# Casting q and k of step 9 inside step 7's block, and loading v of step 10 behind step 9's transpose

## The chip, the cores and the metric

The kernel runs on one NeuronCore of one Trainium2 chip. The metric is the device time of one execution in microseconds (us). The kernel before was run six times: 205.12, 204.30, 204.86, 205.36, 204.22 and 204.88 us, so its median is 204.87 us. One further execution was recorded by the hardware profiler; all views of the profile come from that one.

## The reference

A decaying linear attention over blocks of 64 tokens is followed by a dense layer pair with a GELU between. Inputs are q, k and v (4 batches, 8 heads, 768 tokens, 64 features, float32), one decay `lam` per head, `w_in` (512 x 2048) and `w_out` (2048 x 512). The output is 3072 x 512 in float32.

```python
for b in range(nb):                      # blocks of 64 tokens
    intra = einsum('bhic,bhjc->bhij', qb, kb) * Dmask      # scores under the decay mask
    intra = einsum('bhij,bhjd->bhid', intra, vb)
    inter = einsum('bhid,bhde->bhie', qb * lam_pow, kv_state)
    out[block b] = intra + inter
    kv_state = lam**block * kv_state + einsum('bhsd,bhse->bhde', kb * rev_pow, vb)
x = out.transpose(0, 2, 1, 3).reshape(B * S, H * D)
h = x @ w_in
g = 0.5 * h * (1 + tanh(c * (h + 0.044715 * h**3)))
return g @ w_out
```

## The kernel before

**Steps.** The attention is cut into 24 steps, numbered 0 to 23. A step is one batch, 256 tokens and four of the eight heads; step 2i and step 2i + 1 hold the two halves of the heads for the same tokens, and three such pairs make up a batch. The 256 tokens of a step are treated as two chunks of 128 (called c = 0 and c = 1). What a step needs before its matmuls is made in these parts:

- `load_step(s)` issues three DMAs of 256 KB, for q, k and v of the step, from SyncE's queue (SP, line 69). Each of the three has four buffers. Steps 0 to 8 are loaded by the code at the top; from step 6 on, `prep_v(s)` ends with `load_ahead(s + 3)`, so `prep(6)` loads step 9, `prep(7)` step 10, `prep(8)` step 11 and `prep(9)` step 12.
- `prep_qk(s)` casts q to fp16 with its decay on VectorE (line 240) and k to fp16 on ScalarE (line 245). For steps from `FIRST_DMA_T = 9` on it then issues a DMA on SP that transposes both (line 249) into the tile `qkT`. Steps before 9 are transposed by TensorE in `stage_t` (line 261) and copied out of PSUM on ScalarE or VectorE.
- `prep_v(s)` casts v to fp16 with its decay on GpSimd (POOL, line 230). `prep(s)` is `prep_qk(s)` followed by `prep_v(s)`.

**Blocks.** `R(n, s)` puts out the matmuls of two steps that are one apart: `scores(n)` (q times k of step n, line 290, which reads `qkT` of step n); then `products(n, s)`, which is k times v of step n (line 325), masked scores times v of step s (line 339), and the carried state times q of step s (line 348), followed by the copies to `xT` on ScalarE (line 367); then `causal(n)`, the masking of step n's scores on VectorE (line 299); and `update(n, 0)`. `U(n)` is `update(n, 1)`. An `update(n, c)` adds to the state on VectorE (lines 384 and 387) and then spreads it into a tile `u` on POOL (line 394). The state matmuls of step s in `products(n, s)` read `u` of (s - 2, 1) for chunk 0 and `u` of (s, 0) for chunk 1.

**Filler.** Between the blocks, `fill(n)` puts out the next n pieces of the dense layers: matmuls with `w_in` into `Hps` (line 422) with a GELU on ScalarE (line 426), and the second layer's products `MA`, `MB`, `MC`, `MD` (line 493), which use sums of `gT` made on VectorE (line 469).

**Order.** Every instruction is pinned (`pin`): each engine, and SP's DMA queue, runs its own in the order of the code, and an instruction that waits holds up everything behind it on its engine. Around the change the code reads:

```python
    R(6, 5)
    ...
    R(7, 6)
    U(7)
    prep(9)
    fill(2)
    for n in range(8, NSTEP + 1):
        stage_t(n); prep(n + 2); fill(2); R(n, n - 1); fill(1); U(n); fill(2 or 3)
```

So on SP the order is: the load of step 9, a store of an output tile, the load of step 10, another store, the load of step 11, the transpose of step 9, the load of step 12, the transpose of step 10, the load of step 13. On POOL it is: the `u` tiles of step 7, v of step 9, v of step 10, the two `u` tiles of step 8, v of step 11. The `u` of (8, 0) is read in `R(9, 8)`, which also has the `scores(9)` that read the transpose of step 9.

Of the kernel before, what the change touches and what calls it, by code (L numbers as in the profile page):

```python
# [15 lines left out]
def kernel(  # L16
# [22 lines left out]
    FIRST_DMA_T = 9  # L39
# [18 lines left out]

    ld32 = {}

    def load_step(s):
        b, r = divmod(s, 2 * NSB)
        sb, half = divmod(r, 2)
        ts = []
        for nm, src in (("q", q), ("k", k), ("v", v)):
            t = ld.tile([P, HH, 2, D], FP32, tag=nm + "32", name=f"{nm}32_{s}")
            rows = src[b, half * HH : (half + 1) * HH, sb * SB : (sb + 1) * SB, :]
            queue = nc.scalar if (nm, s) == ("v", 0) else nc.sync
            pin(queue.dma_start(out=t[:].rearrange("p h j d -> p h (j d)"),  # L69
                                in_=rows.rearrange("h (p j) d -> p h (j d)", j=2)))  # L70
            ts.append(t)
        ld32[s] = ts

    w_in16 = w16p.tile([P, NC, DFF], FP16)
    w_out16 = w16p.tile([P, NF, DM], FP16)
# [67 lines left out]
    def load_ahead(s):  # L143
        if s < NSTEP:
            load_step(s)
# [50 lines left out]
    def odd(hs):  # L196
        pin(nc.vector.tensor_tensor(dq[:, hs, 1], dq[:, hs, 0], lam_bc[:, hs], ALU.mult))

    def inverse(hs):
        pin(nc.vector.reciprocal(dv[:, hs], dq[:, hs]))  # L200
# [16 lines left out]
    def prep(s):  # L217
        prep_qk(s)
        prep_v(s)

    def wide(t):
        return t.rearrange("p j h d -> p h j d")

    def decay(t, s):
        hs = halves[s % 2]
        return t[:, hs, :].unsqueeze(3).to_broadcast([P, HH, 2, D])

    def prep_v(s):
        tv = a16p.tile([P, 2, HH, D], FP16, tag="v16", name=f"v16_{s}")
        pin(nc.gpsimd.tensor_tensor(wide(tv[:]), ld32[s][2][:], decay(dv, s), ALU.mult))  # L230
        a16[s] = a16[s] + (tv,)
        if s >= 6:
            load_ahead(s + 3)

    def prep_qk(s):
        q32, k32, _ = ld32[s]
        tqk = a16p.tile([P, 2, 2, HH, D], FP16, tag="qk16", name=f"qk16_{s}")
        tq, tk = tqk[:, 0], tqk[:, 1]
        q_eng = nc.gpsimd if s == 3 else nc.vector
        pin(q_eng.tensor_tensor(wide(tq), q32[:], decay(dq, s), ALU.mult))  # L240
        if s == 0:
            inverse(halves[0])
            odd(halves[1])
            inverse(halves[1])
        pin(nc.scalar.activation(out=wide(tk), in_=k32[:], func=AF.Copy))  # L245
        a16[s] = (tq, tk)
        if s >= FIRST_DMA_T:
            o = qkp.tile([P, 2, 2, 2, P], FP16, tag="qkT", name=f"qkT_{s}")
            pin(nc.sync.dma_start_transpose(out=o[:].rearrange("p a j h t -> p (a j h) t"),
                                            in_=tqk[:].rearrange("p a j h d -> p (a j h d)")))  # L250
            qkT[s] = o

    def stage_t(s):
        if s >= FIRST_DMA_T:
            return
        tq, tk = a16[s][:2]
        Tps = ps_M.tile([P, 2, 2, 2, P], FP16, tag="M", name="Tps")
        for i, t in enumerate((tq, tk)):
            for hp in range(2):
                for j in range(2):  # L260
                    pin(nc.tensor.transpose(Tps[:, i, j, hp, :], t[:, j, 2 * hp : 2 * hp + 2, :],  # L261
                                            ident[:]))
        o = qkp.tile([P, 2, 2, 2, P], FP16, tag="qkT", name=f"qkT_{s}")
        if s in (2, 3):
            pin(nc.scalar.activation(out=o[:, 0], in_=Tps[:, 0], func=AF.Copy))
            pin(nc.vector.tensor_copy(out=o[:, 1], in_=Tps[:, 1]))
        elif s in (1, 5, 6, 8):
            pin(nc.scalar.activation(out=o[:], in_=Tps[:], func=AF.Copy))
        else:
            pin(nc.vector.tensor_copy(out=o[:], in_=Tps[:]))  # L270
        qkT[s] = o
# [7 lines left out]
    def half64(i):  # L279
        return slice(64 * i, 64 * i + 64)  # L280
# [3 lines left out]
    def scores(n):  # L284
        o = qkT[n]
        Sps = ps_S.tile([P, 2, 2, 2, P], FP32, tag="S", name="Sps")
        for hp in range(2):
            for jk in range(2):
                for hl, c in TILES:
                    pin(nc.tensor.matmul(  # L290
                        Sps[half64(c), hl, hp, jk, :], o[half64(hl), 1, jk, hp, half64(c)],
                        o[half64(hl), 0, :, hp, half64(c)], start=True, stop=True,
                        skip_group_check=True))
        Ss[n] = Sps

    def causal(n):

        t = ptp.tile([P, 2, 2, 2, P], FP16, tag="PT", name=f"PT_{n}")
        pin(nc.vector.tensor_tensor(  # L299
            t[:].rearrange("p a b c d -> p (a b) (c d)"),  # L300
            Ss.pop(n)[:].rearrange("p a b c d -> p (a b) (c d)"),
            mask[:].unsqueeze(1).to_broadcast([P, 4, 2 * P]), ALU.mult))
        PTs[n] = t

    def products(n, s, banks=None, evacuate=True):


        OK, opened = banks or ([ps_M.tile([P, 512], FP32, tag="M", name=f"OK{c}")
                                for c in range(2)], set())

        def start(c, hl):
            if (c, hl) in opened:
                return False
            opened.add((c, hl))
            return True

        if n is not None:
            _, tk, tv = a16[n]
            last = (n // 2) % NSB == NSB - 1
            for jk in range(2):  # L320
                for hp in range(2):
                    for c, hl in TILES:
                        if c == 1 and last:
                            continue
                        pin(nc.tensor.matmul(  # L325
                            OK[c][half64(hl), 256 + hp * D : 256 + hp * D + D],
                            tk[half64(c), jk, 2 * hp + hl, :], tv[half64(c), jk, 2 * hp + hl, :],
                            start=start(c, hl), stop=(jk == 1), skip_group_check=True))
            Kps[n] = OK
        if s is None:  # L330
            return OK, opened
        sbg, half = divmod(s, 2)
        o = qkT.pop(s)
        PT = PTs.pop(s)
        _, _, tv = a16.pop(s)
        for hp in range(2):
            for jk in range(2):
                for c, hl in TILES:
                    pin(nc.tensor.matmul(  # L339
                        OK[c][half64(hl), hp * P : hp * P + P], tv[half64(c), jk, 2 * hp + hl, :],  # L340
                        PT[half64(c), hl, hp, jk, :], start=start(c, hl), stop=False,
                        skip_group_check=True))
        for c in range(2):
            if c == 0 and sbg % NSB == 0:
                continue
            u = us.pop((s, 0) if c else (s - 2, 1))
            for hp in range(2):
                pin(nc.tensor.matmul(OK[c][:, hp * P : hp * P + P], u[:, hp].rearrange("p l d -> p (l d)"),  # L348
                                     o[:, 0, :, hp, half64(c)], start=False, stop=True,
                                     skip_group_check=True))  # L350
        if evacuate:
            x_out(s, OK)
        return OK, opened

    def x_out(s, OK, second=None):
        sbg, half = divmod(s, 2)
        g, i = group_of[sbg]
        if g not in xT:
            xT[g] = xtp.tile([P, 2, len(groups[g]), 2, SB], FP16, tag="xT", name=f"xT_{g}")
        dst = xT[g][:, half, i]  # L360
        for c in range(2):
            d = dst[:, :, c * P : (c + 1) * P].rearrange("p hp (t j) -> p hp j t", j=2)
            o = OK[c][:, 0:256].rearrange("p (hp j t) -> p hp j t", hp=2, j=2)
            if c == 1 and second is not None:
                pin(second.tensor_copy(out=d, in_=o))
            else:
                pin(nc.scalar.activation(out=d, in_=o, func=AF.Copy))  # L367
# [228 lines left out]
        for _ in range(min(n, len(filler))):  # L596
            filler.pop(0)()

    def R(n, s):
        if n is not None:  # L600
            scores(n)
        products(n, s)
        if n is not None:
            causal(n)
        if s is not None and s % 2 == 1:
            g, i = group_of[s // 2]
            if i == len(groups[g]) - 1 and g > 0:
                queue_group(g)
        if n is not None:
            update(n, 0)  # L610
# [94 lines left out]
    sum_wout(1, 1, DVE)  # L705
    sum_wout(1, 7, DVE)
    fill(2)
    R(7, 6)
    U(7)
    prep(9)  # L710
    fill(2)

    for n in range(8, NSTEP + 1):
# [41 lines left out]
```

## Time and profile before

| | value |
|---|---|
| median of six runs | 204.87 us |
| the profiled execution, its own time | 205.59 us |
| its span in the trace | 203.8 us |
| TensorE matmul busy | 195.1 us (96%) |
| VectorE busy | 145.1 us (71%) |
| ScalarE busy | 108.3 us (53%) |
| GpSimd busy | 66.2 us (32%) |
| transposes by DMA | 15, median 4.6 us from issue to landing |
| loads of q, k, v from SP | 71, medians 4.9, 4.8 and 5.3 us |

Times in the views are microseconds from the start of the span. A timeline row gives start, duration, engine, line, operation, written tile and read tile, how often (x), and in brackets the idle time before it with what ended that. In the chain of waits, each row is a piece of the work that ended last, in order of time. SPq marks an instruction that issues a DMA; its duration is that of the issue, and the landing is told apart. The granted TensorE clock is 1.00.

### The profile page before, as it was taken

The page shows a single profiled execution, that of the slowest core. Times are in us where ns is not written, and L with a number is a line of the kernel's source. Part 1 is how long each engine was busy: PE and PEld are TensorE (multiplying, and loading weights), DVE is VectorE, ACT ScalarE, POOL GpSimd, SP SyncE. Part 2 cuts the span into 40 slices and gives each one's busy share as a digit, 9 for nine tenths or more (in the row PEclk, how much of TensorE's full clock was granted, in tenths as well). Part 3 has the DMA queues.
Part 4 walks back from the last instruction along what each step waited for, and adds up shares of the span by engine and source line. Part 5 has one row for each costly group of instructions (what it writes and reads, how often), then busy time and mean ns, then how long its engine had stood idle before and what let it go on. Part 6 is the DMA issues. An engine that isn't in the chain of part 4 may idle for free.

```text
span 203.8 us, 5650 instructions
## 1 busy us (share of the span) xinstructions
PE 195.1 (96%) x2348; PEld 129.8 (64%) x2348; DVE 145.1 (71%) x281; ACT 108.3 (53%) x205; POOL 66.2 (32%) x80
## 2 busy tenths in 40 slices
PE   6979999999996999999999999999999999999993
PEld 1556544456885888644688654688554788544882
DVE  5896624889999778939997828996739763226553
ACT  3465777375874473477723377632476431566210
POOL 6594132457473533146044304224413101000000
PEclk9999999999999999999999999999999999999999
DMA  6999999999999999599459985775240003300014
GB/s 173 290 330 388 383 387 374 291 285 279 323 244 213 271 250 292 132 272 209 55 157 193 299 191 146 78 177 149 67 106 0 3 0 106 105 0 0 3 42 164
DMA packets 64201, 37.85 MB, mean 186 GB/s; under 512 B 17584, under 2 KB 59568, under 8 KB 64176
## 3 DMA queue, kind: packets, MB, share of 16 engines
q1 hardware_dynamic: 63344, 36.97, 71.3%
q10 hardware_dynamic: 832, 0.52, 0.9%
q8 instruction: 18, 0.29, 0.6%
q14 instruction: 7, 0.06, 0.1%
HBM read 27.26 MB, written 6.29 MB: 165 GB/s over the span
## 4 chain that ended last, share of the span: by engine, by line
PE 81%; DMA 8%; SPq 4%; DVE 3%; ACT 2%; issue 1%
PE Hps L422 36%; PE MD L493 8%; PE MB L493 8%; PE MA L493 7%; PE MC L493 4%; DMA qkT<-qk 4%; SPq L69 4%; DMA wi<-in_moe_w_in_dram 4%; PE Hps L539 3%; PE Sps L290 3%; PE O2ps L437 3%; PE OK L348 3%; PE OK L339 2%; DVE w_sum L128 2%; PE Tps L261 1%; PE OK L325 1%
## 5 line engine op out<-in xcount | busy, mean ns | idle before, releaser
L422 PE MATMUL Hps<-xT,w_in 128*128 128x512 f16 (+1 forms) x416 | 79.1, 346 | 0.0
L426 ACT ACTIVATE gT<-Hps 128x512 f16<-128x512 f32 x88 | 52.1, 597 | 24.5 <-PE Hps L422 23.6
L422 PEld LDWEIGHTS <-w_in 128*128 128x128 f16 x416 | 40.3, 98 | 33.2
L394 POOL TENSOR_TENSOR u<-t,lumask 128x256 f16<-128x256 f32 x40 | 29.2, 734 | 81.9 <-DVE t L387 59.4
L469 DVE TENSOR_TENSOR gs<-gT 128x512 f16<-128x512 f16 (+1 forms) x74 | 43.0, 641 | 12.7 <-ACT gT L426 12.6
L493 PEld LDWEIGHTS <-gs 128*128 128x128 f16 x400 | 38.7, 98 | 4.4
L299 DVE TENSOR_TENSOR PT<-Sps,mask 128x1024 f16<-128x1024 f32 x24 | 29.2, 1216 | 14.5 <-PE Sps L290 14.5
L230 POOL TENSOR_TENSOR v<-v,dv 128x512 f16<-128x512 f32 x24 | 28.7, 1194 | 6.4 <-DMA v<-in_v_dram 2.8
L367 ACT ACTIVATE xT<-OK 128x256 f16<-128x256 f32 x47 | 18.1, 455 | 19.2 <-PE OK L348 15.8
L500 ACT ACTIVATE m<-MB 128x512 f32<-128x512 f32 x10 | 6.0, 597 | 26.5 <-PE MB L493 26.5
L493 PE MATMUL MA<-w_sum,gT 128*128 128x256 f16 x160 | 19.5, 273 | 0.1
L245 ACT ACTIVATE qk<-k 128x512 f16<-128x512 f32 x24 | 15.0, 626 | 8.3 <-DMA k<-in_k_dram 7.0
L493 PE MATMUL MD<-w_sum,gs 128*128 128x256 f16 x152 | 19.4, 273 | 0.0
L493 PE MATMUL MB<-w_out,gs 128*128 128x256 f16 x160 | 19.1, 273 | 0.0
L493 PEld LDWEIGHTS <-gT 128*128 128x128 f16 x160 | 15.5, 98 | 3.1 <-ACT gT L426 0.5
L240 DVE TENSOR_TENSOR qk<-q,dq 128x512 f16<-128x512 f32 x23 | 16.4, 717 | 0.0
L504 DVE TENSOR_TENSOR o<-MA,m 128x512 f32<-128x512 f32 x10 | 6.9, 685 | 12.0 <-ACT m L500 12.0
L387 DVE SCALAR_TENSOR_TENSOR t<-t,lamu,OK 128x64 f32<-128x64 f32 x64 | 14.7, 272 | 0.6
L437 PE MATMUL O2ps<-w_out,gT 128*128 128x512 f16 x64 | 14.6, 379 | 0.0
L128 DVE TENSOR_TENSOR w_sum<-w_out 128x1024 f16<-128x1024 f16 x10 | 9.0, 936 | 6.3 <-POOL w_out L118 3.5
L290 PEld LDWEIGHTS <-qkT 64*64 64x64 f16 x384 | 6.1, 106 | 10.0 <-issue 4.7
L290 PE MATMUL Sps<-qkT 64*64 64x128 f16 x384 | 10.0, 222 | 2.1 <-DMA qkT<-qk 1.6
(59 smaller groups left out, 159.0 us busy)
## 6 DMA issues: line engine op xcount, KB each, us to landing
q<-in_q_dram SPq DMA_DIRECT2D x24, 256.0 KB, 4.9
k<-in_k_dram SPq DMA_DIRECT2D x24, 256.0 KB, 4.8
v<-in_v_dram SPq DMA_DIRECT2D x23, 256.0 KB, 5.3
out_dram<-o SPq DMA_DIRECT2D x22, 256.0 KB, 3.4
wo<-in_moe_w_out_dram SPq DMA_DIRECT2D x4, 1024.0 KB, 9.6
wi<-in_moe_w_in_dram SPq DMA_DIRECT2D x4, 512.0 KB, 7.6
wi<-in_moe_w_in_dram SPq DMA_DIRECT2D x2, 1024.0 KB, 12.7
v<-in_v_dram ACTq DMA_DIRECT2D x1, 256.0 KB, 4.2
```

The costliest lines, as they stand in the source:

```text
L230: pin(nc.gpsimd.tensor_tensor(wide(tv[:]), ld32[s][2][:], decay(dv, s), ALU.mult))
L240: pin(q_eng.tensor_tensor(wide(tq), q32[:], decay(dq, s), ALU.mult))
L245: pin(nc.scalar.activation(out=wide(tk), in_=k32[:], func=AF.Copy))
L290: pin(nc.tensor.matmul(Sps[half64(c), hl, hp, jk, :], o[half64(hl), 1, jk, hp, half64(c)], o[half64(hl), 0, :, hp, half64(c)], start=True, ...
L299: pin(nc.vector.tensor_tensor(t[:].rearrange("p a b c d -> p (a b) (c d)"), Ss.pop(n)[:].rearrange("p a b c d -> p (a b) (c d)"), mask[:]. ...
L367: pin(nc.scalar.activation(out=d, in_=o, func=AF.Copy))
L394: pin(nc.gpsimd.tensor_tensor(u[:], state[half][:].unsqueeze(2).to_broadcast([P, 2, 2, D]), lumask[:, 2 * half : 2 * half + 2, :].unsqueez ...
L422: pin(nc.tensor.matmul(by_block(Hps[:, i, :]), w_in16[:, c, f * P : (f + 1) * P], x(c), start=(c == 0), stop=(c == NC - 1)))
L426: pin(nc.scalar.activation(out=dst, in_=Hps[:], func=AF.Gelu_apprx_tanh))
L437: pin(nc.tensor.matmul(O2[tau][0][:], gT[:, f % HF, f // HF, tau * P : (tau + 1) * P], w_out16[:, f, :], start=(n == 0), stop=(n == NF - 1)))
L469: pin(nc.vector.tensor_tensor(gsum[m][:, i, :], block(T0, F0, i), block(T1, F1, i), op))
L493: pin(nc.tensor.matmul(dst, lhsT, rhs, start=(i == 0), stop=(i == HF - 1), skip_group_check=True))
```

## The change

The two casts of step 9 and its transpose move from behind `U(7)` into `R(7, 6)`, between `scores(7)` and `products(7, 6)`; `prep_v(9)` stays where it was. The load of v of step 10 is taken out of the load of that step and issued directly behind the transpose of step 9. No instruction is added or removed: it is the order on SP, VectorE and ScalarE that changes.

```diff
-    def load_step(s):
+    def load_step(s, names="qkv"):
...
-        ts = []
+        ts = ld32.setdefault(s, [])
         for nm, src in (("q", q), ("k", k), ("v", v)):
+            if nm not in names:
+                continue
...
     def prep_v(s):
...
         if s >= 6:
-            load_ahead(s + 3)
+            if s + 3 == FIRST_DMA_T + 1:
+                load_step(s + 3, "qk")
+            else:
+                load_ahead(s + 3)
...
     def prep_qk(s):
...
             qkT[s] = o
+            if s == FIRST_DMA_T:
+                load_step(s + 1, "v")
...
-    def R(n, s):
+    def R(n, s, ahead=None):
+
         if n is not None:
             scores(n)
+        if ahead:
+            ahead()
         products(n, s)
...
-    R(7, 6)
+    R(7, 6, lambda: prep_qk(9))
     U(7)
-    prep(9)
+    prep_v(9)
     fill(2)
```

On SP the order becomes: q and k of step 10, the store, the load of step 11, the transpose of step 9, v of step 10, the load of step 12, the transpose of step 10. On VectorE the cast of q of step 9 stands ahead of the masking of step 7; on ScalarE the cast of k of step 9 stands ahead of the copies to `xT` of step 6. POOL keeps its order.

More of the change, by code (lines that the diff above doesn't have):

```diff
@@ L71, in load_step @@
             ts.append(t)
-        ld32[s] = ts
     w_in16 = w16p.tile([P, NC, DFF], FP16)
```

## The prediction

> **What bounds the kernel now.** I read the page first: TensorE's matmuls are busy for 195.1 of 203.8 us, so the time is TensorE's work plus its few stalls, and a change that adds no work can only move a stall. Next the chain of waits, to see whether one lies where the change acts.
>
> ```profile
> 55.94 0.42 PE Hps L422 x4
> 56.36 8.26 DMA qkT<-qk
> 64.62 0.04 issue
> 64.66 0.42 PE Sps L290 x16
> 65.43 0.33 PE OK L348 x4
> ```
>
> One piece of that chain is a transfer: the transpose of step 9 (T9 below), 8.26 us from issue to landing against a median of 4.6 for the fifteen. After it the chain is TensorE again nearly to the end (about 1.6 us of ScalarE and issue near 76 us come from ScalarE's own order). So a shift of TensorE at 65 us should reach the end of the run whole. The timeline of TensorE gives the size.
>
> ```profile
> 61.15 1.91 PE L493 MATMUL MB<-w_out,gs 128*128 128x256 f16 x16
> 64.66 0.42 PE L290 MATMUL Sps<-qkT 64*64 64x128 f16 x16 [1.60 <-DMA qkT<-qk]
> 65.36 0.40 PE L348 MATMUL OK<-qkT,u 128*128 128x128 f16 x4
> ```
>
> `scores(9)` stands idle for 1.60 us. Counted as the chain counts 16 such matmuls (1.75 us for another MB row), MB is through at 62.90 and the stall is 1.76 us. That is all the change can win here. The timeline of SP's queue shows why T9 is late.
>
> ```profile
> 52.29 0.72 SPq L69 DMA_DIRECT2D v<-in_v_dram  x1
> 53.10 0.71 SPq L444 DMA_DIRECT2D out_dram<-o  x1
> 55.32 0.66 SPq L69 DMA_DIRECT2D v<-in_v_dram  x1
> 56.36 4.06 SPq L249 DMA_TRANSPOSE qkT<-qk  x1
> 60.46 0.57 SPq L69 DMA_DIRECT2D q<-in_q_dram  x1
> ```
>
> The rows are v of step 10, a store, v of step 11, T9 and q of step 12. The issue of T9 holds SP for 4.06 us, where the shortest of the fifteen takes 1.23. By the issues' times to landing, v of step 10 lands at 59.0, v of step 11 at 62.1, T9 at 64.62 and q of step 12 at 65.26: the order of issue. In front of T9 the landings follow each other every 0.80 us (59.68, the store, to 62.09 is three loads). The last view is POOL's timeline, for who uses v of step 10.
>
> ```profile
> 59.16 1.04 POOL L230 TENSOR_TENSOR v<-v,dv 128x512 f16<-128x512 f32 x1 [1.05 <-DMA v<-in_v_dram]
> 60.32 1.48 POOL L394 TENSOR_TENSOR u<-t,lumask 128x256 f16<-128x256 f32 x2
> 62.25 1.04 POOL L230 TENSOR_TENSOR v<-v,dv 128x512 f16<-128x512 f32 x1 [0.45 <-DMA v<-in_v_dram]
> ```
>
> These are the cast of v of step 10 (already waiting for its load by 1.05 us), the two `u` tiles of step 8, and the cast of v of step 11. The `u` of (8, 0) is read by the last two matmuls at L348 in `R(9, 8)`, 0.11 us into that group, at 65.47. It is ready at about 61.1, so 4.4 us early.
>
> **The casts.** They cost the same in their new place. On VectorE q of step 9 (about 0.7 us at 55.38) goes ahead of the masking of step 7 (53.48 to 54.69). The masked scores are read at 57.98, so 3.3 us of cover hold a delay of 0.7; without that cover it would cost those 0.7 us. The updates of step 7 end at 56.0 instead of 55.46, and q of step 10 follows where it did. On ScalarE k of step 9 (0.66 us) goes ahead of the copies to `xT` (53.92 to 54.71), which no matmul reads before step 7's are made too, at 59.2; from 55.03 on that engine is as before. k of step 9 was loaded by 53.73, and the casts end by about 54.6, ahead of SP. Taken as nothing; the bounds are 0 and +0.3 us.
>
> **T9.** SP was ready for it at 55.98 and waited for the cast of q (56.2). With one load fewer in front, SP reaches it near 55.2 with both casts done. But I do not read the gain from the issue time: T9's issue ends at 60.42, 1.67 us ahead of the landing of the load in front of it (62.09), and two later ones show the same (T10: 65.08 against 66.92; T11: 68.66 against 70.50). A transpose is let go when what is ahead has drained. What the change takes from ahead is one load, so T9 moves by 0.80 us: issue over at 59.62, landed at 63.82. The bounds are 0 (the gap is lost elsewhere) and more, if T9 lands as closely behind its forerunner as T10 and T11 do (0.89 and 0.97 us, against T9's 2.53): 61.29 + 0.9 = 62.2. Part of those 2.53 may be a transfer of instructions: the DMA view of 62.3 to 63.5 has this row, and the trace's packet starts at 62.39.
>
> ```profile
> q8 instruction: 1, 0.02, 5.2%
> ```
>
> T9's last 256-byte packets start at 62.44, so an earlier T9 may miss it; v of step 10 then stands where T9 stood.
>
> **v of step 10.** It moves past the store, the load of step 11 and T9, and so behind T9's issue. Nothing overtakes in that queue, so it lands as q of step 12 did, 0.64 us behind T9: 63.82 + 0.64 = 64.46, 5.5 us later than now. SP issues it at 59.66, which is 4.80 us before that; q of step 12 took 4.79. Behind its cast on POOL, which now waits, are queued both `u` tiles of step 8 and the cast of v of step 11; TensorE waits for the first. From landing to `u`: 0.16 us to start (59.00 to 59.16), 1.04 for the cast, 0.74 for one `u` (half of 1.48), so 1.94 us, and `u` of (8, 0) is ready at 66.40. The two matmuls that stood at 65.47 now start there: +0.93 us. The stall at `scores(9)` shrinks from 1.76 to 0.96 us (scores at 63.86), and a new one of about 1.7 us comes at L348, 0.7 us further on. This is the sum: 0.93 later than the profiled execution's own 205.59 us. I put it on the median of the runs, 204.87, for 205.8; their spread (204.22 to 205.36) may well hold other lengths of the old stall.
>
> Break-even is a landing at 65.47 - 1.94 = 63.53. The landing's bounds are 62.2 + 0.64 = 62.84 and, if T9 does not move, 65.26. The cast's bounds are 1.04 and 1.49 (both in POOL's timeline), `u`'s 0.61 and 0.90. The ends are 62.84 + 0.16 + 1.04 + 0.61 = 64.65 (-0.82 us) and 65.26 + 0.16 + 1.49 + 0.90 = 67.81 (+2.34 us). I take the row of q of step 12, the one load that stands right behind T9.
>
> The load of step 12, T10 and all after it see the same bytes ahead as before: nothing. T10 lands at 67.8 and is used at 70.9, and step 8's second `u` and v of step 11 have over 5 us.
>
> **Two rules of the Trainium skill.** The page "DMA: Bandwidth & Descriptors", section "Anatomy of one DMA", gives about 2.0 us plus bytes over 436 GB/s, an estimate of 2.6 us for 256 KB; that fit is for GpSimd's queue. It speaks against my forecast: issued at 59.66 the load would land at 62.26, `u` would be ready at 64.20, and the change would win 1.27 us. The shortest load of this trace took 3.0 us on an empty queue and the one behind T9 4.79, so I stay with the rows.
>
> The page "SBUF — State Buffer", on the pair of ports that VectorE and GpSimd share, says that a VectorE instruction with two SBUF inputs and a GpSimd one that reads SBUF exclude each other for a whole instruction. The trace has v of step 9 at 1.49 us beside the cast of q of step 10, which took 1.10 instead of 0.7. The late cast of v of step 10 would meet q of step 11 (63.76 to 64.44 now); by the rule it could lose those 0.68 us, by the row 0.45, for +1.6 or +1.4 us. I leave it to the range, since the two may just miss each other.
>
> **The rivals.** *Faster:* T9 and the load both miss the instruction transfer and land early. For it: T10 and T11 land 0.9 us behind their forerunners, and loads behind a transpose on a quieter queue take 3.3 us (85.80 to 89.08), which from 59.66 is 62.94. Against it: the DMA engines are at 9 tenths in nearly all slices of the page up to here, and the transfer at 62.39 would find the load where it found T9. Its time: -0.82 us by the early end, 204.05; the full -1.76 (203.1) would need a landing by about 61.8, when the load's packets have hardly begun. *Even:* T9 misses it, the load lands near 63.5, one stall replaces the other: 204.9. *Slower,* the forecast: the wait of POOL for v of step 10 takes the place of TensorE's wait for T9, and it decides from a landing later than 63.53. *The change does not do what it says,* T9 staying where it is because the queue only fills again in front of it: the load lands at 65.26, `u` at 67.20, +1.73 us, 206.6; against it, the freed 0.80 us is bytes that no other transfer takes.
>
> **How the numbers follow.** What a measurement can tell from no change is about 0.3%, 0.61 us: 204.26 to 205.48. Forecast (204.87 + 0.93) 0.48; T9 not moved 0.08; even 0.24; faster 0.20. The forecast's own range is 205.2 to 206.5 (+0.3 to +1.6), and 0.03 of it falls below 205.48. So faster 0.20, within 0.27, slower 0.53. Across both signs the range goes from 203.9, just beyond the early end, to 206.5.
>
> **What would show it.** In the changed profile: T9 issued near 55.2 and landed near 63.8; v of step 10 issued near 59.7 and landed near 64.5, with a POOL row at L230 waiting about 6 us for it; a stall on TensorE ahead of the last L348 matmuls of `R(9, 8)`, ended by POOL's `u`; nothing new in VectorE's or ScalarE's rows. I am wrong if L348 waits for nothing, if v of step 10 lands before 63, or if the difference arises after 77 us.

## The result and the profile after

The changed kernel takes 205.57 us (median of 15 runs, 205.28 to 205.99); the kernel before, run beside it and earlier, 204.57 us (34 runs, 204.19 to 205.61). The ratio is 1.0048, with a 95% interval of 1.0037 to 1.0059: about 1.0 us slower. The profiled execution took 205.95 us, with a span of 204.1 us.

Lines have moved by a few: L348 of before is L354, L290 is L296, L493 is L499, L230 is L231, L249 is L253, L394 is L400. First come rows of TensorE's timeline of the changed kernel (start, duration, engine, line, operation, tiles, count, idle time before and what ended it):

```profile
61.75 1.91 PE L499 MATMUL MB<-w_out,gs 128*128 128x256 f16 x16
63.59 0.42 PE L296 MATMUL Sps<-qkT 64*64 64x128 f16 x16
64.29 0.28 PE L354 MATMUL OK<-qkT,u 128*128 128x128 f16 x2
65.83 0.28 PE L354 MATMUL OK<-qkT,u 128*128 128x128 f16 x2 [1.25 <-POOL u L400]
```

`scores(9)` no longer waits. The four state matmuls are now torn in two: the pair of chunk 0 runs, and the pair of chunk 1 stands until POOL has made `u` of (8, 0). Counted from start to start, the second pair would have followed at 64.40 (0.11 behind the first) and comes at 65.83, so the new wait is worth 1.43 us. POOL's timeline shows what it waited for:

```profile
57.82 1.22 POOL L231 TENSOR_TENSOR v<-v,dv 128x512 f16<-128x512 f32 x1
63.79 1.41 POOL L231 TENSOR_TENSOR v<-v,dv 128x512 f16<-128x512 f32 x1 [4.75 <-PE MB L499]
65.16 1.18 POOL L400 TENSOR_TENSOR u<-t,lumask 128x256 f16<-128x256 f32 x2
```

These rows are the casts of v of steps 9 and 10 and the two `u` tiles of step 8. The middle one stood idle for 4.75 us; the view names MB as its releaser because that came last by its events, but what it reads, v of step 10, landed at 63.63, 0.16 us ahead of its start. The second profile of this kernel names the load itself (4.93 us, and 1.26 us at L354), and in the kernel before the same cast ran at 59.16, ahead of all of MB. That the order on POOL is what holds `u` can be read from VectorE's row of the state that the `u` of (8, 0) is made from:

```profile
60.38 0.46 DVE L393 SCALAR_TENSOR_TENSOR t<-t,lamu,OK 128x64 f32<-128x64 f32 x2
```

It was done at 60.84, while POOL stood idle, and the `u` still ran only at 65.16, behind the cast. On SP:

```profile
54.62 0.96 SPq L71 DMA_DIRECT2D v<-in_v_dram  x1
55.75 2.58 SPq L253 DMA_TRANSPOSE qkT<-qk  x1
58.46 0.49 SPq L71 DMA_DIRECT2D v<-in_v_dram  x1
59.00 0.50 SPq L71 DMA_DIRECT2D q<-in_q_dram  x1
```

They are v of step 11, the transpose of step 9 (T9), v of step 10 and q of step 12. T9 holds SP for 2.58 instead of 4.06 us and lands at 61.20, 0.92 behind v of step 11 (60.28). In VectorE's and ScalarE's rows I found nothing new that anyone waits for.

### The profile page after: what moved, and what is told of

It is laid out like the page before. It is cut to its first block, busy times and chain, and to the rows that moved or that the text cites. A ratio compares the mean times of both kernels' runs of the same rounds, so it can differ in the third digit from the quotient of the medians.

```text
span 204.1 us, 5649 instructions
## 1 busy us (share of the span) xinstructions
PE 195.8 (96%) x2348; PEld 130.8 (64%) x2348; DVE 143.8 (70%) x281; ACT 108.2 (53%) x205; POOL 65.7 (32%) x80
## 4 chain that ended last, share of the span: by engine, by line
PE 92%; DVE 2%; issue 2%; POOL 1%; ACT 1%; POOLq 0%
PE Hps L428 37%; PE MB L499 9%; PE MA L499 8%; PE MD L499 8%; PE O2ps L443 7%; PE MC L499 4%; PE Sps L296 4%; PE Hps L545 3%; PE OK L354 3%; PE OK L345 3%; PE Tps L267 2%; PE idle L156 2%; PE OK L331 1%; POOL dq L190 1%; DVE PT L305 1%
## 5 line engine op out<-in xcount | busy, mean ns | idle before, releaser
L400 POOL TENSOR_TENSOR u<-t,lumask 128x256 f16<-128x256 f32 x40 | 28.9, 728 | 80.4 <-DVE t L393 57.4
L475 DVE TENSOR_TENSOR gs<-gT 128x512 f16<-128x512 f16 (+1 forms) x74 | 42.1, 628 | 12.7 <-ACT gT L432 12.6
L499 PEld LDWEIGHTS <-gs 128*128 128x128 f16 x400 | 38.7, 98 | 4.4
L231 POOL TENSOR_TENSOR v<-v,dv 128x512 f16<-128x512 f32 x24 | 28.4, 1183 | 9.7 <-PE MB L499 4.8
L499 PE MATMUL MA<-w_sum,gT 128*128 128x256 f16 x160 | 19.5, 273 | 0.1
L499 PE MATMUL MD<-w_sum,gs 128*128 128x256 f16 x152 | 19.4, 273 | 0.0
L499 PE MATMUL MB<-w_out,gs 128*128 128x256 f16 x160 | 19.1, 273 | 0.0
L249 ACT ACTIVATE qk<-k 128x512 f16<-128x512 f32 x24 | 15.0, 625 | 6.4 <-DMA k<-in_k_dram 6.4
L499 PEld LDWEIGHTS <-gT 128*128 128x128 f16 x160 | 15.5, 98 | 3.2 <-ACT gT L432 0.5
L129 DVE TENSOR_TENSOR w_sum<-w_out 128x1024 f16<-128x1024 f16 x10 | 8.2, 865 | 7.2 <-ACT w_out L117 3.7
L296 PEld LDWEIGHTS <-qkT 64*64 64x64 f16 x384 | 6.3, 108 | 8.5 <-issue 4.4
L345 PE MATMUL OK<-PT,v 64*64 64x128 f16 x384 | 10.2, 218 | 0.6 <-DVE PT L305 0.6
```

The source lines that it names most:

```text
L345: pin(nc.tensor.matmul(OK[c][half64(hl), hp * P : hp * P + P], tv[half64(c), jk, 2 * hp + hl, :], PT[half64(c), hl, hp, jk, :], start=star ...
L400: pin(nc.gpsimd.tensor_tensor(u[:], state[half][:].unsqueeze(2).to_broadcast([P, 2, 2, D]), lumask[:, 2 * half : 2 * half + 2, :].unsqueez ...
L475: pin(nc.vector.tensor_tensor(gsum[m][:, i, :], block(T0, F0, i), block(T1, F1, i), op))
L499: pin(nc.tensor.matmul(dst, lhsT, rhs, start=(i == 0), stop=(i == HF - 1), skip_group_check=True))
```

## The experiments

Theory A is the forecast's: v of step 10 lands late behind T9, its cast waits on POOL, and `u` of step 8, queued behind the cast, holds TensorE. Theory B, a rival: the early casts delay masking, updates or copies on VectorE and ScalarE. The diffs are against the changed kernel.

**E1, the casts alone.** The load of v of step 10 is back in its old place.

```diff
         if s >= 6:
-            if s + 3 == FIRST_DMA_T + 1:
-                load_step(s + 3, "qk")
-            else:
-                load_ahead(s + 3)
+            load_ahead(s + 3)
...
-            if s == FIRST_DMA_T:
-                load_step(s + 1, "v")
```

> The casts and the transpose of step 9 stand in R(7, 6) as in the changed kernel, but v of step 10 is loaded in its old place, ahead of the load of step 11. Theory A (the changed kernel is slower because the cast of v of step 10 waits on POOL for its late load and holds back the u tile of step 8): that load lands near 59.5 again, no wait of L354 for u in R(9, 8), so at or below the kernel before: 203.5 to 204.7, with at most the old stall at scores(9). Theory B (the early casts on VectorE and ScalarE delay the masking, the state updates or the copies and with them TensorE): as slow as the changed kernel, 205.3 to 205.8.

Measured: 204.51 us, 0.9982 of before (0.9960 to 1.0005). No wait for `u`; a wait of 0.77 us at `scores(9)` in its profile, T9 landing at 63.90:

```profile
63.95 0.42 PE L291 MATMUL Sps<-qkT 64*64 64x128 f16 x16 [0.77 <-DMA qkT<-qk]
64.64 0.40 PE L349 MATMUL OK<-qkT,u 128*128 128x128 f16 x4
```

The early casts do not make the kernel slower, so B falls; whether they win anything is not told apart from nothing.

**E2, the load alone.** T9 and its casts stay behind `U(7)`.

```diff
-    R(7, 6, lambda: prep_qk(9))
+    R(7, 6)
     U(7)
-    prep_v(9)
+    prep(9)
```

> The casts and the transpose of step 9 stand behind U(7) as in the kernel before; only the load of v of step 10 is moved behind that transpose. Theory A: the load is issued behind a transpose that starts near 56.3, so it lands at 63.6 to 65.3 and u of step 8 is ready no earlier than in the changed kernel: 205.3 to 207.0, with a wait of L354 for POOL. Theory B: no early casts, so as the kernel before, 204.3 to 204.9.

Measured: 205.96 us, 1.0051 of before (1.0027 to 1.0074), as much as the whole change. Its TensorE timeline has the same new wait without the early casts:

```profile
63.13 0.42 PE L296 MATMUL Sps<-qkT 64*64 64x128 f16 x16
65.37 0.29 PE L354 MATMUL OK<-qkT,u 128*128 128x128 f16 x2 [1.26 <-POOL u L400]
```

Here T9 was issued at 56.47 and landed at 60.76, and v of step 10 landed at 63.35. So T9 needs no early casts to be in time.

**E3, the cast behind `U(8)`.** The loads up to step 12 keep their order as in the change, and the load of step 13 goes out later, with the cast; POOL makes both `u` tiles of step 8 first.

```diff
         if n + 2 < NSTEP:
-            prep(n + 2)
+            (prep_qk if n == 8 else prep)(n + 2)
...
             U(m)
+        if n == 8:
+            prep_v(n + 2)
```

> The changed kernel, with the cast of v of step 10 put behind U(8), so that on POOL both u tiles of step 8 go ahead of it; all loads and transposes keep their order on SP but for the load of step 13, which goes out with that cast. Theory A: the wait of L354 (1.25 us in the profile of the changed kernel) is gone, and so is the wait at scores(9): 203.7 to 204.4, at or below the kernel before. Theory B: the early casts are still there, 205.3 to 205.8.

Measured: 204.45 us, 0.9980 of before (0.9958 to 1.0003), just above the expected range. TensorE waits neither at `scores(9)` nor at L354. A row of TensorE's timeline, then POOL's:

```profile
64.32 0.40 PE L354 MATMUL OK<-qkT,u 128*128 128x128 f16 x4
```

```profile
61.01 1.42 POOL L400 TENSOR_TENSOR u<-t,lumask 128x256 f16<-128x256 f32 x2 [1.94 <-DVE t L393]
62.39 2.93 POOL L231 TENSOR_TENSOR v<-v,dv 128x512 f16<-128x512 f32 x2
```

The `u` tiles now wait for VectorE's state alone, and the cast comes after. With the load still issued behind T9 and the cast moved, the loss is gone. But the load itself landed earlier here, at 61.89 against 63.63 in the changed kernel, early enough for `u` in the old order too (an estimate: with the 2.15 us from landing to `u` of the changed kernel, `u` would be ready at 64.04, and the second pair stood at 64.43). So this run alone does not show that the order on POOL is what costs; the changed kernel's rows do, where the state was done at 60.84 and `u` stood behind the cast.

**E4, another load behind T9.** v of step 11 takes the place of v of step 10.

```diff
-            if s + 3 == FIRST_DMA_T + 1:
+            if s + 3 == FIRST_DMA_T + 2:
...
-                load_step(s + 1, "v")
+                load_step(s + 2, "v")
```

> The changed kernel with v of step 11, not v of step 10, loaded behind the transpose of step 9. As many bytes are taken from ahead of the transpose; v of step 11 is cast on POOL behind the u tiles of step 8 and used some 12 us later. Theory A: the transpose lands as early as in the changed kernel (about 61 to 62), no wait for u: 203.5 to 204.4. Theory B: 205.3 to 205.8, as the changed kernel.

Measured: 204.33 us, 0.9975 of before (0.9950 to 1.0000). T9 lands at 61.08, v of step 11 at 62.10; no wait on TensorE in `R(9, 8)`:

```profile
64.51 0.40 PE L354 MATMUL OK<-qkT,u 128*128 128x128 f16 x4
```

T9 lands as early as in the change, and no one waits for the load that went behind it.

**E5, further back.** v of step 10 goes behind the load of step 12.

```diff
             else:
                 load_ahead(s + 3)
+            if s == FIRST_DMA_T:
+                load_step(s + 1, "v")
...
-            if s == FIRST_DMA_T:
-                load_step(s + 1, "v")
```

> The changed kernel with v of step 10 put still further back on SP, behind the load of step 12 (three loads later). Theory A (POOL's wait for that load holds the u tile of step 8): it lands about 3 x 0.8 = 2.4 us later, near 66, and the wait of L354 for u grows from 1.25 us by about as much: 206.8 to 208.5. Theory B (early casts): no change to the changed kernel, 205.3 to 205.8.

Measured: 209.99 us, 1.0255 of before (1.0229 to 1.0281). The load lands at 65.97, as expected, and the wait grows by 2.33 us, as expected, but the time is above the expected range: it grows by about 4.4 us over the changed kernel (3.6 between the two profiled executions, 209.59 and 205.95). Its TensorE timeline, then the stretches of its span (length; busy time and count of each engine; granted clock; DMA):

```profile
67.79 0.29 PE L354 MATMUL OK<-qkT,u 128*128 128x128 f16 x2 [3.58 <-POOL u L400]
67.92 1.04 PE L499 MATMUL MC<-w_sum,gs 128*128 128x256 f16 x8
68.79 3.37 PE L499 MATMUL MD<-w_sum,gs 128*128 128x256 f16 x16
```

```profile
67.80:69.00 1.20, 1.20 (x12) 1.10 (x13) 0.01 (x1) 0.46 (x1) 1.20 (x2) 1.00 1.22 283
69.00:70.00 1.00, 1.00 (x7) 0.69 (x5) 1.00 (x3) 0.00 (x0) 0.88 (x2) 0.52 1.82 254
70.00:71.00 1.00, 1.00 (x7) 0.70 (x5) 0.06 (x1) 0.00 (x0) 0.80 (x2) 0.50 0.78 177
71.00:72.00 1.00, 1.00 (x7) 0.67 (x6) 0.00 (x0) 0.00 (x0) 0.82 (x1) 0.50 1.22 289
72.00:74.00 2.00, 2.00 (x18) 1.71 (x17) 1.29 (x2) 0.72 (x2) 0.00 (x0) 0.89 0.66 154
74.00:76.00 2.00, 2.00 (x56) 1.62 (x54) 0.62 (x1) 1.54 (x4) 0.00 (x0) 1.00 0.78 259
```

Sixteen MD matmuls take 3.37 instead of 1.91 us: the granted clock is 0.50 after the wait. Set against the changed kernel's profile, TensorE is 1.97 us later at L354 (it was 0.36 us earlier ahead of the wait) and 3.63 us later by the next `scores` (74.91 against 71.28), so 1.66 us more come from the clock. The rest of the 4.4 us goes with the clock too: the mean granted clock was 0.992 in three of the six executions (209.10 to 209.82 us) and 0.984 in the other three (210.16 to 210.35), while in every execution of the changed kernel it was 0.997 to 1.000.

**E6, behind step 11, ahead of T9.** The load is late by three loads and a store, but not behind T9.

```diff
             else:
                 load_ahead(s + 3)
+            if s + 3 == FIRST_DMA_T + 2:
+                load_step(s + 2, "v")
...
-            if s == FIRST_DMA_T:
-                load_step(s + 1, "v")
```

> The changed kernel with v of step 10 loaded behind the load of step 11 and ahead of the transpose of step 9, so three loads and a store later than in the kernel before, but not behind the transpose. Theory A: what costs is a landing past the point from which u of step 8 comes late (about 62.1, from L354 at 64.4 less the 2.2 us that cast and u took); here it lands near 60 to 61.5, so no wait for u, 203.9 to 204.9. If any delay of that load costs, 205.2 or more.

Measured: 204.57 us, 0.9992 of before (0.9971 to 1.0013). The load lands at 60.56; its cast waits 1.19 us on POOL, but `u` is in time and TensorE does not wait:

```profile
64.77 0.40 PE L354 MATMUL OK<-qkT,u 128*128 128x128 f16 x4
```

So the load may be late up to a point. Behind T9 it was past that point in both profiles of the changed kernel and in E2 (63.35 to 63.89), though not in E3 (61.89).

**The kernel before, profiled again.** E3 and E4, without any wait here, were only 0.4 to 0.5 us faster than before, though the first profile had shown 1.60 us of wait.

> The kernel before, profiled a second time. The kernels without any wait at scores(9) or L354 were only 0.4 to 0.5 us faster than it, though its first profile shows 1.60 us of wait at scores(9). If that profile was a long case, this one shows a wait of 0.2 to 0.9 us, with a time of 204.3 to 205.0; if the wait is always about 1.6 us, then the two kernels without it lose about 1 us elsewhere.

> The kernel before, profiled a third time, for the spread of the wait at scores(9): 0.2 to 1.7 us, with the landing of the transpose of step 9 moving with it; a transfer of instructions that starts within 1 us ahead of that landing in the long cases.

> The kernel before, profiled a fourth time: one profile of three had a wait of 1.60 us at scores(9), two had none. Theory A has no say in this one; a time near 204.3 to 204.7 goes with no wait, one above 205.2 with a long one.

Measured: 204.62, 204.71 and 205.10 us, spans of 202.8, 202.9 and 203.3, and in none of them a wait at `scores(9)`. The expectations of a shorter wait failed: there was none. TensorE's timeline of the second profile of before:

```profile
61.51 1.91 PE L493 MATMUL MB<-w_out,gs 128*128 128x256 f16 x16
63.34 0.42 PE L290 MATMUL Sps<-qkT 64*64 64x128 f16 x16
64.05 0.40 PE L348 MATMUL OK<-qkT,u 128*128 128x128 f16 x4
```

T9 landed at 63.20, 61.35 and 61.79 in these three, against 64.62 in the first. In the second it was 2.50 us behind v of step 11, as late as in the first (2.53), but loads and TensorE stood otherwise to each other, and T9 was in time by a little; in the other two it was 0.98 and 1.04 behind. The expected mark of a late T9, a transfer of instructions within 1 us ahead of its landing, did not hold: where T9 was late, the transfer started 2.2 us ahead of the landing (62.39, 60.99), where it was not, 0.7 us (60.67, 61.06). The fourth profile's time, 205.10 without a wait, shows that a run's time alone does not tell of this stall: its TensorE was simply later by then (MB at 62.00).

**The changed kernel, profiled again.**

> The changed kernel, profiled a second time. Theory A: no wait at scores(9), and again a wait of L354 for u of 0.8 to 1.7 us, with v of step 10 landing 2 us or more behind the transpose of step 9; time 205.3 to 206.0.

Measured: 206.04 us, just above the expected range, no wait at `scores(9)`, 1.26 us at L354, the load landing at 63.89, 2.61 behind T9.

## Why the prediction was right, step by step

The forecast of 205.8 us, the direction and the mechanism held (measured 205.57); the terms of the sum were off on both sides and made up for each other, so that the number came this close is in part luck.

- **A shift at 65 us reaches the end.** Nearly. Against the second profile of before, TensorE is 1.66 us later at L354, 0.24 of it from the start of the run, and 1.31 us later at the end of the span. 0.23 us go at once: in the three profiles of before without the stall, the second half of MD waits for VectorE's last sum (MD takes 2.16 instead of 1.91 us), and a later TensorE does not. Another 0.09 go in the `Hps` matmuls behind it.
- **The casts cost nothing.** Held: E1 is not slower, and E2 without them is as slow as the change.
- **T9 moves by 0.80 us, to 63.82.** Mis-sized. It landed at 61.20, 0.92 us behind its forerunner, as the early bound had it after T10 and T11. I had carried over the 2.53 us of the one profile; the forerunner too came 1.01 us earlier (60.28) than the 61.29 taken. Much of this need not be the change: against the third and fourth profile of before, in which T9 was not late either (61.35 and 61.79), it landed 0.15 to 0.59 us earlier.
- **v of step 10 lands 0.64 us behind T9, at 64.46.** Mis-sized the other way: 2.43 us behind T9, at 63.63, 5.17 us after its issue at 58.46 (4.80 expected). The row of q of step 12 had followed a T9 that was itself late; in the later three profiles of before, that load comes 0.67, 2.18 and 2.13 us behind T9.
- **1.94 us from landing to `u`.** 2.15: 0.16 to the start, 1.41 for the cast (1.23 in the second profile; 1.04 taken, 1.49 the bound), 0.61 for `u` (0.74 taken), less 0.04 by which the rows of the cast and of `u` overlap.
- **The stalls.** The new one was put at 1.7 and is 1.43 us. The old one was put at 1.76 us, with 0.96 left. In the changed kernel none is left, and in three of four profiles of before there was none to remove. This was the step that failed in the working: a wait seen in one execution was taken for the kernel's. I had noted that other runs may hold another length of it, and drew nothing from that.

As measured, the sum is +1.43 for the new wait, nothing for the old one, -0.23 where VectorE's sum no longer holds MD, and -0.09 behind that: +1.11 us, against 0.76 to 1.21 us by the interval of the ratio on 204.57. Had the old wait always been 1.76, the measured new one would have made the kernel 0.33 us faster instead. The break-even landing, put at 63.53, is then 62.25 (64.40 less 2.15): E6 (60.56) and E3 (61.89) are under it, the changed kernel (63.63) and E5 (65.97) are over, and the wait rises by 2.33 us for 2.34 us of landing between the last two.

Of the rivals, *even* and *faster* needed an early load and an old wait to win from; by the rows of each of its two profiles the load came about 1.4 us too late, and the old wait was not there as a rule. *The change does not do what it says* had T9 where it was and the load at 65.26; T9 landed at 61.20 and the load at 63.63, so it falls in that form, but how much of T9's move the change itself made is not shown.

The estimate of 2.6 us for a 256 KB load, from the Trainium skill's page "DMA: Bandwidth & Descriptors" (section "Anatomy of one DMA", a fit for GpSimd's queue), does not describe this queue: the load took 5.17 and 5.26 us in the two profiles. The page "SBUF — State Buffer" (section "Summary: rules for kernel authors") has a GpSimd instruction that reads SBUF blocked until a VectorE one with two SBUF inputs that started first is through. The traces agree: the sum of `gs` at 63.62 to 64.30 (two SBUF inputs) was under way when the cast started at 63.79, with 0.51 us to go, and the cast took 0.37 us longer than 1.04; in the second profile it was 0.19 with 0.33 to go, and in before 0.45 with 0.58 to go (the cast of v of step 9 at 56.63, beside the cast of q of step 10). Of the 216 casts of v behind 44 us in the twelve profiles, the 84 that met no such instruction took 1.03 or 1.04 us, and the other 132 took longer by what was left of it, less 0.13 or 0.14.

What stays open is why the load behind T9 lands 2.4 to 2.6 us behind it in the changed kernel and E2, but 1.02 us in E3 and E4, and why T9 itself is late in some profiles. In E3 the transfer of instructions starts at 62.90, after the load's landing at 61.89; in the changed kernel at 60.58, between the load's issue and its landing. In E4 it starts at 61.31, ahead of the landing of v of step 11 at 62.10, and it is q of step 12 that comes late (2.24 us behind). All twelve profiles have the same pattern: between 61 and 67 us one landing comes 2.07 to 2.61 us behind the one ahead of it, all others there 1.6 at most, and that one comes 2.2 to 3.1 us after such a transfer starts. That fits a transfer which holds up one DMA engine for the about 1 us it lasts, and with it whatever is next in line there, but no run moved it on purpose, so it is argued, not shown.

E4 has the best time of all (0.9975, up to 1.0000) with E3 next; both clearly undo the loss. That either beats the kernel before is likely but not settled, since there is usually no wait here to remove.

## What to carry to other kernels

Before you push a load back in a queue, find the first instruction that reads it, and then read what is queued behind that instruction on its engine: the price is set by the most urgent work there, not by when the loaded data are themselves needed (v of step 10 is multiplied some 7 us after the `u` that it held up). If something has to go behind a transpose, choose the load whose reader comes after the urgent work (E4), or let the urgent work go first on the reader's engine (E3). And take a stall for the kernel's only after a second and third profile: the one that this change set out from was in one of four.

## What the runs showed of the hardware that was not expected

A wait of TensorE cost more than its length when it grew: after waits of 1.25 us (changed kernel) and 1.60 us (first profile of before) the granted clock stayed at 1.00, but after the 3.58 us of E5 it was 0.50 from about 69 us to past 72, and 1.66 us were lost on top of the wait. The clock did not fall at once: MC, right behind the wait, still ran at full rate (1.04 us for eight). The Trainium skill's page "TensorE: Matmul & The Clock Gate" (section "HAM oscillation — how this bites in real kernels") has the clock halved by waits longer than about 3.4 us; these three lengths agree with that, and no run here lies between 1.60 and 3.58.
